# One transfer for each tile of tokens, and a new order of the first loads

## The chip, the cores and the metric

The kernel runs on one core of one Trainium2 chip. The metric is the time on the device, in microseconds (us); smaller is better.

## What is computed

The input is x, 2048 tokens of 576 numbers. Each token is normalized (mean 0, variance 1, 1e-5 added under the root) to xn. The output adds three things:

```python
xn = _layernorm(x, axis=-1)
return x + _A_ref(xn, ...) + _B_ref(xn, w1, w2)
# _B_ref: h = silu(xn @ w1)      w1 is 576 x 4608
#         out = h @ w2           w2 is 4608 x 576
# _A_ref: K[d,l] = Re(sum_n C dB exp(dt A l)), 128 states for each d
#         y = causal convolution of xn with K over the 2048 tokens, + xn * Dskip
```

All is float32. The kernel writes float32 operands of TensorE as a high and a low part (`xh`, `xl`; `w1h`, `w1l`; `gh`, `gl`) and multiplies high by high, high by low and low by high.

## The kernel before, in words

**Tiles of tokens.** The 2048 tokens are 16 tiles `j` of 128. A tile is not a run of neighbours: token number = 64 n + (16 times a quarter) + j, with n from 0 to 31 and four quarters. A tile in SBUF has 128 partitions, 32 for each quarter. In DRAM the 32 rows of one quarter lie 64 tokens apart, and the four quarters 16 tokens apart. `quarters` (L73) yields the four quarters with the queue that each is to use; `load_x` (L163) and `store` (L175) issue one transfer of 32 rows for each. Tiles 0 and 1 are loaded one by one, from SyncE's (SP) and ScalarE's (ACT) queues in turn, the others in pairs `j, j+1` of 4.6 KB a row.

**The feed-forward part** (`ffn`, L242) runs over two halves of the tokens (tiles 0 to 7, 8 to 15), nine chunks of 512 of the 4608 hidden columns, and two blocks of four tiles. `up` (L303) multiplies w1 into 128 hidden columns at a time, ScalarE applies silu (`gf`) and makes `gh`, VectorE (DVE) makes `gl`; `down` (L323) multiplies w2 and DVE adds to the accumulator `acc` (L346), which starts as x itself. `load_w1` (L250) fetches 256 columns of w1 as `w1r`: rows 0 to 511 in one transfer (L257) and rows 512 to 575 twice, to both halves of the partitions (L258, L259). For the very first columns it cuts these three in two by columns, for the two queues. `split_w1` (L271) makes `w1h` on ScalarE (L279) and `w1l` on DVE (L281). The last seven chunks of the second half use a Winograd-like scheme (`wino_ffn`, L468).

**The convolution** is done beside it, as a generator `side` (L1050) that `weave` interleaves with `ffn`: phase 0 (load, `norm`, transpose), the table of K (`natural`, `kgen`), a transform (`spread`, `spectral`) through DRAM buffers `d1u`, `d1k`, `d2`, and at the end `conv` (L1032), which adds the result to a tile: for tiles 0 to 7 through `yt` and an adding store, for tiles 8 to 15 into the same PSUM bank as the last `down`.

**Order.** Each engine runs its instructions in order. A scheduler in the framework sets the order from the code and from hints: `behind(ins)` puts an instruction behind another, `tc.high_priority()` pulls it forward. `norm` (L180) holds tile 1's statistics (`bn_stats`, L188) behind tile 0's normalized tile (`pins["xn"]`). Each queue issues its transfers in order.

**The end.** After the last `down`, pairs 8, 10 and 12 and the tiles 14 and 15 are stored from the two queues (L1111 to L1114).

Of the kernel before, what the change touches and what calls it, by code (L numbers as in the profile page):

```python
# [13 lines left out]
ALU = mybir.AluOpType  # L14
# [3 lines left out]
P = 128  # L18
# [4 lines left out]
NJ = 16  # L23
NKT = 4
HD = D // 2
# [16 lines left out]
def kernel(  # L42
# [21 lines left out]
    nc = tc.nc  # L64
# [2 lines left out]
    WINO_C = 2  # L67


    xv = x.rearrange("b (n q2 q1 j) d -> q1 q2 n (b j) d", q2=2, q1=2, j=NJ)  # L70
    ov = out.rearrange("b (n q2 q1 j) d -> q1 q2 n (b j) d", q2=2, q1=2, j=NJ)

    def quarters(v, engines):  # L73

        for q in range(4):
            yield slice(32 * q, 32 * q + 32), v[q // 2, q % 2], engines[q % len(engines)]

    dram = ctx.enter_context(tc.tile_pool(name="dram", bufs=1, space=DRAM))
    d1u = dram.tile([32 * P, D], F32, name="d1u")
# [10 lines left out]
    s4 = None  # L90
# [19 lines left out]
    acc = {}  # L110
# [21 lines left out]
    pairs = {}  # L132
    held = []
    pins = {}
    wino = {}

    def behind(ins):
        return tc.issue_after(ins) if ins is not None else nullcontext()

    def spread(up):  # L140

        s1 = up.tile([P, 2, P], F32R, name="s1", bufs=1)
        nc.gpsimd.dma_start(s1, cs1)
        for j in range(NJ):
            src = up.tile([P, D], F32, tag="xr", name="xr")
            nc.sync.dma_start(src, dxn[:, j])
            for m in range(2):
                lo, hi = slice(64 * m, 64 * m + 64), slice(64 - 64 * m, 128 - 64 * m)
                u1 = up.tile([P, D], F32, tag="u1", name="u1")
                sp = up.tile([P, D], F32R, tag="sp", name="sp")  # L150
                nc.scalar.copy(sp[lo, :], src[lo, :])
                nc.vector.tensor_sub(sp[hi, :], src[lo, :], sp[lo, :])
                for h in range(2):
                    hs = slice(h * HD, (h + 1) * HD)
                    pu = pss.tile([P, 512], F32, tag="pss", name="pu")
                    nc.tensor.matmul(pu[:, :HD], s1[:, 0, :], sp[:, hs], start=True, stop=False)
                    nc.tensor.matmul(pu[:, :HD], s1[:, 1, :], sp[:, hs], start=False, stop=True)
                    nc.scalar.copy(u1[:, hs], pu[:, :HD])  # L158
                nc.gpsimd.dma_start(  # L159
                    d1u.rearrange("(p m j) d -> m j p d", m=2, j=NJ)[m, j], u1)  # L160
                yield j

    def load_x(j, pool, tag, engines):  # L163

        t = pool.tile([P, 2, D], F32, tag=tag, name=f"{tag}{j}")
        for i in range(j, j + 2, 1 if j == 0 else 2):
            for ps, v, eng in quarters(xv, engines):
                if j == 0:
                    eng.dma_start(t[ps, i], v[:, i])
                else:  # L170
                    eng.dma_start(t[ps], v[:, j:j + 2])
        pairs[j] = t
        return t[:, 0, :], t[:, 1, :]

    def store(t, j, engines, **more):  # L175

        for ps, v, eng in quarters(ov, engines):
            eng.dma_start(v[:, j:j + 2] if len(t.shape) > 2 else v[:, j], t[ps], **more)

    def norm(p0, js, xs):  # L180

        n = len(js)
        st = p0.tile([P, 2, 2, 6], F32, tag="st", name="st")
        mv = p0.tile([P, 2, 2], F32, tag="mv", name="mv")
        for i in range(n):
            for h in range(2):
              with behind(pins["xn"] if js[0] == 1 else None):
                nc.vector.bn_stats(out=st[:, i, h, :], in_=xs[i][:, h * HD:(h + 1) * HD])  # L188
            nc.vector.bn_aggr(out=mv[:, i, :], in_=st[:, i, :, :])
        sd = p0.tile([P, 2], F32, tag="sd", name="sd")  # L190
        mb = p0.tile([P, 2], F32, tag="mb", name="mb")
        nc.vector.tensor_scalar(sd[:, :n], mv[:, :n, 1], 1e-5, None, op0=ALU.add)
        pins["sd"] = nc.gpsimd.tensor_tensor(sd[:, :n], sd[:, :n], mhalf[:, :n], op=ALU.pow).ins
        xn = p0.tile([P, 2, D], F32, tag="xn", name="xn") if js[0] < 8 else pairs[js[0]]
        for i, j in enumerate(js):
            if j % 2 == 0 or j < 4:
                pins["xn"] = nc.vector.tensor_scalar(xn[:, i, :], xs[i], mv[:, i, 0:1], sd[:, i:i + 1],
                                                 op0=ALU.subtract, op1=ALU.mult).ins
            else:
                nc.vector.scalar_tensor_tensor(mb[:, i:i + 1], mv[:, i, 0:1], -1.0, sd[:, i:i + 1],  # L200
                                               op0=ALU.mult, op1=ALU.mult)
                pins["xo"] = nc.scalar.activation(xn[:, i, :], xs[i], AF.Identity,
                                                  scale=sd[:, i:i + 1], bias=mb[:, i:i + 1]).ins
        return xn

    def phase0(p0, js):
        j0 = js[0]
        if j0 < 8:
            xs = load_x(j0, accp, "acc", (nc.sync, nc.scalar) if j0 == 0 else (nc.sync,))
            acc.update(zip(js, xs))  # L210
            yield
        else:
            xs = load_x(j0, p0, "xj", (nc.sync,))
        if j0:
            with behind(pins["xt1"] if j0 == 2 else None):
                turned(p0, js, norm(p0, js, xs))
        else:
            xn = [norm(p0, (j,), (xj,)) for j, xj in zip(js, xs)]
            last = pins["xn"]
            for j in js:  # L220
                turned(p0, (j,), xn[j], None if j else last)
                pins[f"xt{j}s"] = pins["xt_s"]
# [19 lines left out]
    def ffn():  # L242
# [7 lines left out]
        def load_w1(half, c, t):  # L250

            f = c * FT + t
            first = half == 0 and c == 0
            r1 = (pa if first and t else w1x if t and w1x else wp).tile([P, 5, 2 * P], F32, tag="w1r", name="w1r", bufs=1)
            for eng, a, e in ((nc.scalar, 0, P), (nc.sync, P, 2 * P)) if first and t == 0 else ((nc.sync, 0, 2 * P),):
                fs = slice(f * P + a, f * P + e)
                eng.dma_start(r1[:, 0:4, a:e], w1[0:512, fs].rearrange("(k p) f -> p k f", p=P))  # L257
                eng.dma_start(r1[0:64, 4, a:e], w1[512:576, fs])  # L258
                pins["load"] = eng.dma_start(r1[64:128, 4, a:e], w1[512:576, fs]).ins  # L259
            R1[half, c, t] = r1  # L260

        def need_w1(half, c, t):
# [60 lines left out]
        def down(blk, jj, terms=None):  # L323
# [22 lines left out]
                    nc.vector.tensor_add(acc[j][:, hs], po[:, :HD], acc[j][:, hs])  # L346
            if half == 0 and c == NCH - 1:
                if j % 2:
                    store(pairs[j - 1], j - 1, (nc.gpsimd,))
                    acc[7 + j], acc[8 + j] = load_x(7 + j, accp, "acc", (nc.gpsimd,))  # L350

        def next_xt(b):
            xt = new_xt(2 + b)
# [628 lines left out]
    def tail():  # L982

        def last(j):
            y = yp.tile([P, 2, D], F32, tag="yt", name="yt", bufs=2)
            py = [[pool.tile([P, 512], F32, tag=tag, name="py") for pool, tag in pools]
                  for pools in (((ps2, "ps2"), (pss, "pss")), ((pss, "pss"),) * 2)]
            conv((j, j + 1), py)
            for i in range(2):
                for h in range(2):  # L990
                    nc.scalar.copy(y[:, i, h * HD:(h + 1) * HD], py[i][h][:, :HD])
                conv_load(j + i + AHEAD)
            store(y, j, (nc.gpsimd,), accum_op=ALU.add)

        steps = [(tail_at[0] + j * tail_at[1], conv_load, j) for j in range(AHEAD)]
        steps += [(tail_at[2] + j * tail_at[3], last, j) for j in range(0, 8, 2)]
        for at, f, j in sorted(steps, key=lambda v: v[0]):
            yield at
            with behind(pins["load"]):
                f(j)  # L1000
# [31 lines left out]
    def conv(js, banks):  # L1032

        ys = [yss.pop(j) for j in js]
        first = pins["pe"]
        for n in range(8 * len(js)):
            i, q1, q2, h = n // 8, n // 4 % 2, n // 2 % 2, 1 - n % 2
            o = 64 * q1 + 32 * q2
            rows = slice(64 * h, 64 * h + 64)
            with tc.high_priority() if n else nullcontext(), behind(first):  # L1040
                mm = nc.tensor.matmul(banks[i][h][o:o + 32, :HD], s4[rows], ys[i][rows, 2 * q2 + q1],
                                      start=True, stop=True, tile_position=(64 * h, o), skip_group_check=True)
            if n == 0:
                first = mm.ins
# [64 lines left out]
        next(g)  # L1109
    weave(fg, 276, sd)  # L1110
    for j in range(8, 14, 2):  # L1111
        store(pairs[j], j, (nc.sync, nc.scalar))
    for j in (14, 15):
        store(acc[j], j, (nc.sync, nc.scalar))  # L1114


def _hi_lo(a):
# [75 lines left out]
```

## Time and profile before

| what | value |
|---|---|
| time, median of 3 runs | 1107.63 us (1107.56 to 1108.49) |
| time of the profiled execution | 1108.0 us, of which the span of its instructions is 1106.1 |
| TensorE (PE) busy | 1089.5 us, 98% of the span |
| VectorE (DVE) / ScalarE (ACT) / GpSimd (POOL) busy | 950.6 / 722.6 / 141.5 us |
| granted TensorE clock | 0.999 |
| moved by transfers | 173.67 MB, mean 157 GB/s |

PE's busy share leaves out the start, where it waits for the first data, and the end, where only stores run. A busy PE is not a PE at its peak: ends of matmuls are modelled and overlap.

### The profile page before, as it was taken

The page shows a single profiled execution, that of the slowest core. Times are in us where ns is not written, and L with a number is a line of the kernel's source. Part 1 is how long each engine was busy: PE and PEld are TensorE (multiplying, and loading weights), DVE is VectorE, ACT ScalarE, POOL GpSimd, SP SyncE. Part 2 cuts the span into 40 slices and gives each one's busy share as a digit, 9 for nine tenths or more (in the row PEclk, how much of TensorE's full clock was granted, in tenths as well). Part 3 has the DMA queues.
Part 4 walks back from the last instruction along what each step waited for, and adds up shares of the span by engine and source line. Part 5 has one row for each costly group of instructions (what it writes and reads, how often), then busy time and mean ns, then how long its engine had stood idle before and what let it go on. Part 6 is the DMA issues. An engine that isn't in the chain of part 4 may idle for free.

```text
span 1106.1 us, 23074 instructions
## 1 busy us (share of the span) xinstructions
PE 1089.5 (98%) x9101; PEld 986.5 (89%) x9101; DVE 950.6 (86%) x1615; ACT 722.6 (65%) x1283; POOL 141.5 (13%) x246
## 2 busy tenths in 40 slices
PE   6999999999999999999999999999999999999998
PEld 5989999898998888898999899999999998999787
DVE  6699989999999999999999997988888888886323
ACT  4475457677777676767667656877778777785320
POOL 1112100000000000000330001111111111111220
PEclk9999999999999999999999999999999999999999
DMA  8536552355263535457974246456545655554984
GB/s 261 157 123 205 168 165 94 118 149 153 84 176 108 138 125 132 154 120 254 240 196 89 84 92 193 146 167 179 158 152 176 182 173 150 177 161 109 248 216 111
DMA packets 163100, 173.67 MB, mean 157 GB/s; under 512 B 88608, under 2 KB 128816, under 8 KB 162352
## 3 DMA queue, kind: packets, MB, share of 16 engines
q1 hardware_dynamic: 137360, 105.02, 34.6%
q0 software_dynamic: 24272, 65.38, 19.4%
q10 hardware_dynamic: 1360, 1.80, 0.7%
q8 instruction: 72, 1.18, 0.5%
q14 instruction: 36, 0.29, 0.1%
HBM read 109.64 MB, written 62.60 MB: 156 GB/s over the span
## 4 chain that ended last, share of the span: by engine, by line
PE 78%; DVE 12%; ACT 3%; DMA 3%; issue 2%; SPq 0%; POOL 0%; ACTq 0%; DVEq 0%
PE po L341 34%; PE ph L311 16%; PE pb L468 6%; PE pc L468 3%; PE kp L888 2%; PE pk L1022 2%; PE pb L1022 2%; PE pu L1022 2%; PE pa L468 2%; PE ph L313 1%; PE ph L312 1%; PE z L903 1%; DMA kl<-d1k 1%; DVE acc L346 1%; DVE th L829 1%
## 5 line engine op out<-in xcount | busy, mean ns | idle before, releaser
L341 PE MATMUL po<-w,gh 128*128 128x288 f32 x2304 | 474.3, 296 | 0.7 <-DVE acc L346 0.7
L341 PEld LDWEIGHTS po<-w,gh 128*128 128x128 f32 x2304 | 375.1, 188 | 16.6 <-issue 3.3
L341 PE MATMUL po<-w,gl 128*128 128x288 f32 x1152 | 333.5, 295 | 0.0
L341 PEld LDWEIGHTS po<-w,gl 128*128 128x128 f32 x1152 | 214.9, 188 | 1.7
L346 DVE TENSOR_TENSOR acc<-po,acc 128x288 f32<-128x288 f32 x296 | 129.8, 451 | 54.5 <-PE po L341 53.2
L311 PE MATMUL ph<-xh,w1h 128*128 128x512 f32 (+1 forms) x368 | 99.7, 388 | 1.4 <-ACT gf L319 1.0
L311 PE MATMUL ph<-xl,w1h 128*128 128x512 f32 (+1 forms) x368 | 98.2, 384 | 0.0
L311 PE MATMUL ph<-xh,w1l 128*128 128x512 f32 (+1 forms) x368 | 98.0, 383 | 0.0
L319 ACT ACTIVATE gf<-ph 128x512 f32<-128x512 f32 (+1 forms) x92 | 53.0, 579 | 51.3 <-PE ph L313 31.5
L311 PEld LDWEIGHTS ph<-xl,w1h 128*128 128x128 f32 x368 | 68.0, 191 | 13.4
L311 PEld LDWEIGHTS ph<-xh,w1l 128*128 128x128 f32 x368 | 66.6, 189 | 12.0
L311 PEld LDWEIGHTS ph<-xh,w1h 128*128 128x128 f32 x368 | 65.0, 191 | 11.7 <-ACT gf L319 1.6
L845 ACT ACTIVATE c<-th,magic 128x1040 f32<-128x1040 f32 x36 | 42.0, 1168 | 40.6 <-DVE C L866 26.5
L159 POOL DMA_DIRECT2D d1u<-u x32 | 17.6, 550 | 393.9 <-ACT u L158 392.5
L847 ACT ACTIVATE c<-th 128x1040 f32<-128x1040 f32 x36 | 38.7, 1074 | 40.7 <-DVE th L846 40.6
L321 DVE TENSOR_TENSOR gl<-gf,gh 128x512 fp32r<-128x512 f32 (+1 forms) x92 | 60.3, 658 | 3.8 <-ACT gh L320 3.6
L927 POOL DMA_DIRECT2D m<-in_cm_dram x64 | 34.0, 533 | 216.0 <-PE pu L1022 135.8
L320 ACT CAST gh<-gf 128x512 fp32r<-128x512 f32 (+1 forms) x92 | 55.1, 602 | 8.7 <-PE po L341 7.7
L485 DVE TENSOR_TENSOR gl<-gf,gh 128x512 fp32r<-128x512 f32 x56 | 37.8, 688 | 23.4 <-ACT gh L484 23.0
L865 DVE TENSOR_TENSOR S<-th,C 128x1024 f32<-128x1024 f32 x36 | 43.8, 1218 | 7.4 <-ACT th L848 7.3
L846 DVE SCALAR_TENSOR_TENSOR th<-c,th 128x1040 f32<-128x1040 f32 x36 | 44.3, 1232 | 0.3 <-ACT c L845 0.3
L829 DVE TENSOR_TENSOR th<-vt,fT 128x1040 f32<-128x1040 f32 x36 | 44.3, 1233 | 0.2
(269 smaller groups left out, 2371.0 us busy)
## 6 DMA issues: line engine op xcount, KB each, us to landing
w1r<-in_B_w_dram SPq DMA_DIRECT2D x35, 512.0 KB, 3.9
dw<-w SPq DMA_DIRECT2D x28, 576.0 KB, 4.8
w<-dw POOLq DMA_DIRECT2D x28, 576.0 KB, 5.9
w2r<-in_B_w_dram SPq DMA_DIRECT2D x44, 288.0 KB, 4.8
d1u<-u POOLq DMA_DIRECT2D x32, 288.0 KB, 2.9
d1k<-stage SPq DMA_DIRECT2D x18, 512.0 KB, 6.5
ul<-d1u SPq DMA_DIRECT2D x32, 288.0 KB, 3.0
kl<-d1k SPq DMA_DIRECT2D x32, 288.0 KB, 3.6
```

Of the source, the lines that this page charges most:

```text
L311: nc.tensor.matmul(ph, w[:, kt, :], v[:, kt, a:e], start=n + kt == 0, stop=False)
L319: nc.scalar.activation(gf, ph, AF.Silu)
L320: pins["gh"] = nc.scalar.copy(gh, gf).ins
L321: pins["gl"] = nc.vector.tensor_sub(gl, gf, gh).ins
L341: pins["pe"] = nc.tensor.matmul(po[:, :HD], gs[g][:, js], ws[:, w, hs], start=n == 0 and j not in begun, stop=n == 3 * len(terms) - 1, ski ...
L346: nc.vector.tensor_add(acc[j][:, hs], po[:, :HD], acc[j][:, hs])
L468: pins["pe"] = nc.tensor.matmul(dst, a[:, kt], v[:, kt], start=start and n == 0, stop=stop and n == 5, skip_group_check=True).ins
L829: nc.vector.tensor_mul(split(th), row(vt[:, 0:65], 65), col(fT, i, 65))
L845: nc.scalar.activation(c65, th, AF.Identity, bias=magic)
L846: nc.vector.scalar_tensor_tensor(th, c65, MAGIC, th, op0=ALU.subtract, op1=ALU.subtract)
L865: nc.vector.tensor_mul(ov3, t[:, :, 0:64].rearrange("n d (x y) -> n d x y", y=32), mv3)
L1022: nc.tensor.matmul(dst, st, mv[:, hs], start=n == 0, stop=n == 3 * len(terms) - 1)
```

## The change

It replaces the four quarter transfers of a tile by one, renumbers the quarters so that they stand in natural order, and so changes the patterns of `d1u` and `conv` (same rows, same bytes). It takes the first loads off ScalarE's queue, brings the last 64 rows of w1 to both halves of the partitions by one transfer that reads them twice, places tile 1's statistics behind tile 0's variance, and stores the last tiles whole from ScalarE's queue, tile 15 in two halves by columns from two queues.

```diff
-    xv = x.rearrange("b (n q2 q1 j) d -> q1 q2 n (b j) d", q2=2, q1=2, j=NJ)
-    ov = out.rearrange("b (n q2 q1 j) d -> q1 q2 n (b j) d", q2=2, q1=2, j=NJ)
-    def quarters(v, engines):
-        for q in range(4):
-            yield slice(32 * q, 32 * q + 32), v[q // 2, q % 2], engines[q % len(engines)]
+    xv = x.rearrange("b (n q j) d -> q n (b j) d", q=4, j=NJ)
+    ov = out.rearrange("b (n q j) d -> q n (b j) d", q=4, j=NJ)
...
-                    d1u.rearrange("(p m j) d -> m j p d", m=2, j=NJ)[m, j], u1)
+                    d1u.rearrange("(e m q j) d -> m j e q d", m=2, q=2, j=NJ)[m, j], u1)
...
-    def load_x(j, pool, tag, engines):
+    def load_x(j, pool, tag, eng):
         t = pool.tile([P, 2, D], F32, tag=tag, name=f"{tag}{j}")
-        for i in range(j, j + 2, 1 if j == 0 else 2):
-            for ps, v, eng in quarters(xv, engines):
-                if j == 0:
-                    eng.dma_start(t[ps, i], v[:, i])
-                else:
-                    eng.dma_start(t[ps], v[:, j:j + 2])
+        if j == 0:
+            for i in range(2):
+                eng.dma_start(t[:, i], xv[:, :, i])
+        else:
+            eng.dma_start(t, xv[:, :, j:j + 2])
...
-    def store(t, j, engines, **more):
-        for ps, v, eng in quarters(ov, engines):
-            eng.dma_start(v[:, j:j + 2] if len(t.shape) > 2 else v[:, j], t[ps], **more)
+    def store(t, j, eng, **more):
+        eng.dma_start(ov[:, :, j:j + 2] if len(t.shape) > 2 else ov[:, :, j], t, **more)
...
-              with behind(pins["xn"] if js[0] == 1 else None):
-                nc.vector.bn_stats(out=st[:, i, h, :], in_=xs[i][:, h * HD:(h + 1) * HD])
+                with behind(pins["var"] if js[0] == 1 else None):
+                    nc.vector.bn_stats(out=st[:, i, h, :], in_=xs[i][:, h * HD:(h + 1) * HD])
...
-        nc.vector.tensor_scalar(sd[:, :n], mv[:, :n, 1], 1e-5, None, op0=ALU.add)
+        pins["var"] = nc.vector.tensor_scalar(sd[:, :n], mv[:, :n, 1], 1e-5, None, op0=ALU.add).ins
...
-            for eng, a, e in ((nc.scalar, 0, P), (nc.sync, P, 2 * P)) if first and t == 0 else ((nc.sync, 0, 2 * P),):
-                fs = slice(f * P + a, f * P + e)
-                eng.dma_start(r1[:, 0:4, a:e], w1[0:512, fs].rearrange("(k p) f -> p k f", p=P))
-                eng.dma_start(r1[0:64, 4, a:e], w1[512:576, fs])
-                pins["load"] = eng.dma_start(r1[64:128, 4, a:e], w1[512:576, fs]).ins
+            fs = slice(f * P, (f + 2) * P)
+            eng = nc.sync
+            eng.dma_start(r1[:, 0:4, :], w1[0:512, fs].rearrange("(k p) f -> p k f", p=P))
+            pins["load"] = eng.dma_start(r1[:, 4, :], w1[512:576, fs].unsqueeze(0).broadcast_to([2, 64, 2 * P])).ins
...
-    for j in range(8, 14, 2):
-        store(pairs[j], j, (nc.sync, nc.scalar))
-    for j in (14, 15):
-        store(acc[j], j, (nc.sync, nc.scalar))
+    for j in range(8, 14, 2):
+        store(pairs[j], j, nc.scalar)
+    store(acc[14], 14, nc.scalar)
+    for h, eng in enumerate((nc.scalar, nc.sync)):
+        hs = slice(h * HD, (h + 1) * HD)
+        eng.dma_start(ov[:, :, 15, hs], acc[15][:, hs])
```

How the rows stand in a queue shows the change best. SP's first transfers before; a row names the tile and the tensor it comes from, and the shape written (`acc_104` holds tiles 0 and 1, `acc_171` tiles 2 and 3, `acc_252` 4 and 5, `acc_299` 6 and 7, `w2r` 128 rows of w2):

```order
L169 DMA acc_104<-in_A_u_dram 32x576 x4
L257 DMA w1r<-in_B_w_dram 128x4x128
L258 DMA w1r<-in_B_w_dram 64x128
L259 DMA w1r<-in_B_w_dram 64x128
L257 DMA w1r<-in_B_w_dram 128x4x256
L258 DMA w1r<-in_B_w_dram 64x256
L259 DMA w1r<-in_B_w_dram 64x256
L171 DMA acc_171<-in_A_u_dram 32x1152 x4
L288 DMA w2r<-in_B_w_dram 128x576 x4
L171 DMA acc_252<-in_A_u_dram 32x1152 x4
L171 DMA acc_299<-in_A_u_dram 32x1152 x4
L257 DMA w1r<-in_B_w_dram 128x4x256
```

And now, the same place (`acc_160` holds tiles 2 and 3, `acc_238` 4 and 5, `acc_282` 6 and 7, `xj` the tiles from 8 on):

```order
L163 DMA acc_104<-in_A_u_dram 128x1x576 x2
L249 DMA w1r<-in_B_w_dram 128x4x256
L250 DMA w1r<-in_B_w_dram 128x1x256
L249 DMA w1r<-in_B_w_dram 128x4x256
L250 DMA w1r<-in_B_w_dram 128x1x256
L165 DMA acc_160<-in_A_u_dram 128x1x1152
L279 DMA w2r<-in_B_w_dram 128x576 x4
L165 DMA acc_238<-in_A_u_dram 128x1x1152
L165 DMA acc_282<-in_A_u_dram 128x1x1152
L165 DMA xj_600<-in_A_u_dram 128x1x1152
L165 DMA xj_749<-in_A_u_dram 128x1x1152
L1072 DMA vt<-in_cv_dram 128x69
```

Both tiles, both pieces of w1 and tiles 2 and 3 are now seven transfers in one queue; the four tiles from 8 on stand ahead of the next chunk's w1 (before they stood behind it).

DVE's first rows before, from tile 0's variance to the statistics of tiles 2 and 3 (`st`, `mv`, `sd` are the statistics; rows that name `pt` split a transposed tile):

```order
L192 TENSOR_SCALAR sd<-mv 128x1
L197 TENSOR_SCALAR xn<-acc_104,mv,sd 128x576
L188 BN_STATS st<-acc_104 128x6 x2
L189 BN_AGGR mv<-st 128x2
L192 TENSOR_SCALAR sd<-mv 128x1
L197 TENSOR_SCALAR xn<-acc_104,mv,sd 128x576
L125 TENSOR_TENSOR xl_147<-pt,xh_146 128x4x128
L129 TENSOR_TENSOR x_0_148<-pt_156,x_0_148 64x128
L125 TENSOR_TENSOR xl_147<-pt,xh_146 128x4x128
L129 TENSOR_TENSOR x_0_148<-pt_167,x_0_148 64x128
L281 TENSOR_TENSOR w1l<-w1r,w1h 128x640 x4
L188 BN_STATS st<-acc_171 128x6 x4
```

And now, from the row behind tile 0's variance:

```order
L180 BN_STATS st<-acc_104 128x6 x2
L189 TENSOR_SCALAR xn<-acc_104,mv,sd 128x576
L181 BN_AGGR mv<-st 128x2
L184 TENSOR_SCALAR sd<-mv 128x1
L189 TENSOR_SCALAR xn<-acc_104,mv,sd 128x576
L120 TENSOR_TENSOR xl_136<-pt,xh_135 128x4x128
L124 TENSOR_TENSOR x_0_137<-pt_145,x_0_137 64x128
L120 TENSOR_TENSOR xl_136<-pt,xh_135 128x4x128
L124 TENSOR_TENSOR x_0_137<-pt_156,x_0_137 64x128
L272 TENSOR_TENSOR w1l<-w1r,w1h 128x640
L180 BN_STATS st<-acc_160 128x6 x4
L272 TENSOR_TENSOR w1l<-w1r,w1h 128x640 x3
```

Tile 1's statistics moved ahead of tile 0's normalized tile, as asked; the scheduler also moved the statistics of tiles 2 and 3 ahead of three of the four low parts of w1.

The end of ScalarE's queue before (SP's ends with the same four rows of stores; `acc_6463` is pair 8, `acc_6528` pair 10, `acc_6868` pair 12, `acc_7052` tiles 14 and 15):

```order
L484 CAST gh<-gf 128x512 x2
L178 DMA out_dram<-acc_6463 32x1152 x2
L178 DMA out_dram<-acc_6528 32x1152 x2
L178 DMA out_dram<-acc_6868 32x1152 x2
L178 DMA out_dram<-acc_7052 32x576 x4
```

And now, where SP keeps one row alone, the second half of tile 15:

```order
L475 CAST gh<-gf 128x512 x2
L170 DMA out_dram<-acc_6410 4x32x1152
L170 DMA out_dram<-acc_6469 4x32x1152
L170 DMA out_dram<-acc_6801 4x32x1152
L170 DMA out_dram<-acc_6979 4x32x576
L1107 DMA out_dram<-acc_6979 4x32x288
```

A store that was two rows in each of two queues is one row in one; its shape on the DRAM side has 4 as its first number, where it had 32.

More of the change, by code (lines that the diff above doesn't have):

```diff
@@ L208, in phase0 @@
         if j0 < 8:
-            xs = load_x(j0, accp, "acc", (nc.sync, nc.scalar) if j0 == 0 else (nc.sync,))
+            xs = load_x(j0, accp, "acc", nc.sync)
             acc.update(zip(js, xs))
@@ L212, in phase0 @@
         else:
-            xs = load_x(j0, p0, "xj", (nc.sync,))
+            xs = load_x(j0, p0, "xj", nc.sync)
         if j0:
@@ L348, in down @@
                 if j % 2:
-                    store(pairs[j - 1], j - 1, (nc.gpsimd,))
-                    acc[7 + j], acc[8 + j] = load_x(7 + j, accp, "acc", (nc.gpsimd,))
+                    store(pairs[j - 1], j - 1, nc.gpsimd)
+                    acc[7 + j], acc[8 + j] = load_x(7 + j, accp, "acc", nc.gpsimd)
         def next_xt(b):
@@ L992, in last @@
                 conv_load(j + i + AHEAD)
-            store(y, j, (nc.gpsimd,), accum_op=ALU.add)
+            store(y, j, nc.gpsimd, accum_op=ALU.add)
         steps = [(tail_at[0] + j * tail_at[1], conv_load, j) for j in range(AHEAD)]
@@ L1036, in conv @@
         for n in range(8 * len(js)):
-            i, q1, q2, h = n // 8, n // 4 % 2, n // 2 % 2, 1 - n % 2
-            o = 64 * q1 + 32 * q2
+            i, q, h = n // 8, n // 2 % 4, 1 - n % 2
+            o = 32 * q
             rows = slice(64 * h, 64 * h + 64)
             with tc.high_priority() if n else nullcontext(), behind(first):
-                mm = nc.tensor.matmul(banks[i][h][o:o + 32, :HD], s4[rows], ys[i][rows, 2 * q2 + q1],
+                mm = nc.tensor.matmul(banks[i][h][o:o + 32, :HD], s4[rows], ys[i][rows, q],
                                       start=True, stop=True, tile_position=(64 * h, o), skip_group_check=True)
```

## The prediction

> **What bounds the kernel now.** I read the page first, then the waits of PE, then the chain of waits, and last the timeline and the transfers at both ends. From the page:
>
> ```profile
> span 1106.1 us, 23074 instructions
> PE 1089.5 (98%) x9101; PEld 986.5 (89%) x9101; DVE 950.6 (86%) x1615; ACT 722.6 (65%) x1283; POOL 141.5 (13%) x246
> ```
>
> PE has work for all but 16.6 us. The waits of PE (us in total, times, longest) say where those lie:
>
> ```profile
> PE pt L122 <- DVE xn L197: 8.0, 2, 6.9
> PE ph L311 <- ACT gf L319: 1.0, 3, 0.6
> PE pt L127 <- DVE xl L125: 0.9, 1, 0.9
> ```
>
> Eight are waits for the first normalized tiles; nothing else is over 1. So the change can only act on the start, on the end behind PE's last matmul, or by making a new wait between them. The chain of waits through the start (start, length):
>
> ```profile
> 1.27 2.90 DMA acc<-in_A_u_dram
> 4.29 0.83 DVE st L188 x2
> 6.24 0.03 DVE xn L197
> 6.73 0.82 DVE st L188 x2
> 8.66 0.59 DVE xn L197
> 9.29 1.13 PE pt L122 x4
> 10.45 0.59 ACT xh L123
> 11.08 4.38 PE ph L311 x20
> ```
>
> Tile 0 has landed at 4.17, tile 1's normalized tile follows at 8.66, and `up` starts at 11.08. Rows of the timeline beside it:
>
> ```profile
> 9.59 0.72 ACT L279 CAST w1h<-w1r 128x640 fp32r<-128x640 f32 x1 [0.82 <-DMA w1r<-in_B_w_dram]
> 12.10 3.03 DVE L281 TENSOR_TENSOR w1l<-w1r,w1h 128x640 fp32r<-128x640 f32 x4
> 15.05 1.53 DVE L188 BATCH_NORM_STATS2 st<-acc 128x6 f32<-128x288 f32 x4
> 15.54 0.64 PE L311 MATMUL ph<-xh,w1l 128*128 128x256 f32 x4
> 16.76 0.64 PE L311 MATMUL ph<-xl,w1h 128*128 128x256 f32 x4
> 23.30 2.98 DVE L188 BATCH_NORM_STATS2 st<-acc 128x6 f32<-128x288 f32 x8
> 26.20 1.41 DVE L299 TENSOR_TENSOR w<-w2r,w 128x576 fp32r<-128x576 f32 x2
> ```
>
> Data is there just ahead of use, and PE takes the second low part of w1 at 15.54.
>
> **How a transfer is spread.** All turns on one thing that the trace shows in part. ACT's queue (q10) carries few transfers, so its packets can be counted:
>
> ```profile
> q10 hardware_dynamic: 1360, 1.80, 0.7%
> out_dram<-acc ACTq DMA_DIRECT2D x6, 144.0 KB, 3.6
> acc<-in_A_u_dram ACTq DMA_DIRECT2D x4, 72.0 KB, 3.1
> out_dram<-acc ACTq DMA_DIRECT2D x4, 72.0 KB, 2.3
> w1r<-in_B_w_dram ACTq DMA_DIRECT2D x1, 256.0 KB, 5.0
> w1r<-in_B_w_dram ACTq DMA_DIRECT2D x2, 32.0 KB, 4.5
> ```
>
> Runs of data: 14 transfers of 32 rows, one of 128 rows with 4 pieces, two of 64 rows: 448 + 512 + 128 = 1088. Of the 1360 packets 272 are left, which is 17 transfers times 16. I read this as one closing packet on each of the 16 DMA engines: a transfer of 32, 64 or 128 rows is cut along its rows into 16 equal shares. Every pattern of before has such a number as its slowest dimension. The new ones do not: a tile's 128 tokens are 4 quarters 16 tokens apart, of 32 rows 64 tokens apart, which is no single dimension, so the DRAM side of a load or store is 4 x 32 rows; and the last 64 rows of w1, read twice, are 2 x 64. If the cut still goes along the slowest dimension, it gives 4 shares and 2, and a transfer runs on 4 or 2 of the 16 engines. If it goes along the 128 partitions of the tile, nothing is lost. No row of before shows it; these are the two ends. I take the first, because the shares of before follow the rows of the pattern whatever the size, and a pattern is walked from its slowest dimension.
>
> The Trainium skill, page "DMA: Bandwidth & Descriptors", section "Why a DMA increments its semaphore by 16 and not by 1", says that the number of engines is the largest up to 16 that divides the slowest dimension other than 1 of both patterns. By that rule the loads and stores get 4 engines, the doubled rows 2, and the sum is the one below; with 16 it would be 1105.3. By that rule, the trace agrees as far as it goes (272 = 17 x 16); no run here shows a smaller number.
>
> **What one engine moves.** From the transfers of 1.7 to 4.0 us, and the best slice of the first 30 us (40 slices):
>
> ```profile
> q1 hardware_dynamic: 162, 0.27, 45.7%
> q10 hardware_dynamic: 152, 0.24, 32.5%
> GB/s 0 0 126 308 241 210 125 283 312 150 229 296 210 212 320 240 178 243 320 360 323 335 224 221 237 258 234 320 406 424 401 335 384 382 311 249 239 203 234 246
> ```
>
> 0.51 MB in 78.2% of 16 engines times 2.3 us is 17.7 KB/us for each; 424 GB/s over 16 is 26.5. In the first stretch two queues share an engine; after the change one queue has it, so I take 24, nearer the upper end.
>
> **The start, step by step,** on the engine that serves both the tiles and the doubled rows (closing left out). Traffic begins at 1.8 (third slice of 0.75 us). A tile is 295 KB, 74 on each of 4 engines, 3.1 us: tile 0 in at 4.9, tile 1 at 7.9 (before: 4.17, and 5.5 or so). The first w1 piece is 33 KB a share (1.4) and 66 KB of doubled rows on each of 2 engines (2.7): 12.0. The second piece: 16.1. Tiles 2 and 3, 590 KB, 147 a share, 6.1: 22.3. Four w2 pieces at 0.8: 25.3. Tiles 4 and 5: 31.5; 6 and 7: 37.6.
>
> What waits: DVE's statistics of tile 1 now stand ahead of tile 0's xn, so both wait for tile 1; `up` starts near 14, 3 late. That is soon swallowed: the statistics of tiles 2 and 3 now stand behind the first low part of w1, and the other three low parts are queued behind them. 22.3 + 1.5 (statistics) + 0.8 (a quarter of 3.03) = 24.6, against 15.54 for the matmul that wants it: 9.1 late. Next, PE has then stood for about 6 us. At the start its first 20 matmuls took 4.38 us, later ones 0.64 for 4 less overlap, about 0.12 each; if it must start slowly again, that is 2 more. Last, the statistics of tiles 4 to 7 (23.30 before) come at 32.4 and find 4 and 5 but wait from 33.9 to 37.6 for 6 and 7, with the low parts of w2 (26.20) queued behind; half of that reaches PE, 2. Start: 13. The bounds: at 26.5 KB/us and without the two additions 7; at 17.7, with them, 25. Below 7 the engines' number must be other than 4. The freed ACT queue and the earlier tile-1 statistics gain nothing here: the transfers are late.
>
> **Between.** Each later w1 load has its doubled rows on 2 engines: 2.7 us in place of two 64-row transfers on 16 (8 KB a share, 0.35), so 2.4 later. It counts only where a load is waited for; the chain shows two such places behind the start:
>
> ```profile
> 61.05 3.37 DMA w1r<-in_B_w_dram
> 297.25 3.60 DMA w1r<-in_B_w_dram
> ```
>
> I take 2 x 2.4 = 5; bounds 0 (all covered) and 8 chunks x 2.4 = 19. The patterns of `d1u` and `conv` move the same rows as before; their slowest dimension is 64, so 0. POOL's stores and reloads of tiles are issued fewer to one queue that is busy 13% of the time; their later landing is covered by tens of us. If the adding stores of `yt` crowd the `ys` loads, up to 5 more.
>
> **The end.** DVE's last sums and SP's stores:
>
> ```profile
> 1096.69 0.46 DVE L346 TENSOR_TENSOR acc<-po,acc 128x288 f32<-128x288 f32 x1 [0.34 <-PE po L341]
> 1099.65 0.46 DVE L346 TENSOR_TENSOR acc<-po,acc 128x288 f32<-128x288 f32 x1 [0.35 <-PE po L341]
> 1101.24 0.46 DVE L346 TENSOR_TENSOR acc<-po,acc 128x288 f32<-128x288 f32 x1 [0.35 <-PE po L341]
> 1084.92 17.79 SPq L178 DMA_DIRECT2D out_dram<-acc  x10
> 1092.64 10.07 SPq L178 DMA_DIRECT2D out_dram<-acc  x8
> ```
>
> Pair 8 goes out at 1084.9, pair 10 at 1092.6, pair 12 at 1097.2, tile 14 at 1100.1, tile 15 by 1101.7. On 4 engines a pair takes 6.1, a tile 3.1. With 1.1 from issue to traffic (0.75 to 1.8 at the start): 1086.0 to 1092.1; 1093.7 to 1099.8; pair 12 waits for that, to 1105.9; tile 14 to 1109.0; tile 15 to 1112.1. Before, the last bytes went at about 1104, 2 ahead of the span's end, so the end is 8 later. Stores alone, 1086 to 1104, bound it:
>
> ```profile
> q10 hardware_dynamic: 479, 1.18, 28.2%
> q1 hardware_dynamic: 461, 1.10, 22.6%
> ```
>
> 2.28 MB in 50.8% of 16 x 18 us is 15.6 KB/us: by that 20 later; at 26.5, 7.
>
> **Sum.** 13 + 5 + 8 = 26 on a span of 1106.1, so 1132 and 1134 with the 1.9 around it. The profiled execution was 1108.0, the median 1107.63; against the median 1133.
>
> **Rivals.** *Sixteen shares after all: faster.* Then tile 0 (295 KB at 16 x 17.7) is in at 2.9 plus closing, some 0.9 ahead of 4.17; tile 1's statistics begin when tile 0's variance ends and no more at 6.73, and its xn 0.5 earlier (8.66): 1.4 at the start. At the end one issue (0.45, from 10.07 for 8 and their waits) and half the bytes of tile 15 go: 0.9. 1107.6 - 2.3 = 1105.3. It decides from the point where tile 1 lands before 5.5. For it: more rows a transfer, fewer issues. The skill's page, section "Rules for kernel authors", says to use one 128-partition transfer in place of halves; by that the time is this rival's, 1105.3. Against it: the 4 and 2 above. *Four shares, but the start covered* (an engine over 26.5 KB/us with few others at work, PE slowed by little): only the end stays, 1107.6 + 8 = 1115.6. For it: fewer than 16 engines leave more of the memory to each. Against: tiles 2 and 3 alone would need 10 us less.
>
> **How the numbers follow.** Forecast 0.70 (its own range 1118 to 1150: start 7 to 20, between 0 to 8, end 7 to 12, not all at one end); everything at the slow bounds, over 1150, 0.04; the covered start 0.10 (1112 to 1118); sixteen shares 0.16. The range 1112 to 1150 leaves out 0.16 and 0.04. A measurement of this kernel tells about 0.2% (2.2 us) from no change; the gain of 2.3 lies on that line, so 0.16 falls half to faster, half to same.
>
> **What would show it.** Right: in the transfers, the first tile's landing at about 5 and tile 1's at 8, w1's doubled rows landing some 2.5 behind the rest; DVE's third group of statistics waiting on a transfer until past 20; PE waiting 5 us or more for the low part of w1; stores still moving 7 us or more behind DVE's last sum. Wrong: tile 1 in by 5.5, `up` starting before 11, the last store done within 2.5 of the last sum.

## The result, and the profile after

The changed kernel takes 1191.24 us (median of 6, 1190.43 to 1199.73) against 1107.82 for the kernel before (median of 6): a ratio of 1.0763, 95% interval 1.0734 to 1.0793. The direction is the forecast's; the loss is 83 us where 25 were forecast, and the time lies above the range.

The page of the changed kernel, the lines that answer to those shown of before:

```profile
span 1189.1 us, 22898 instructions
PE 1106.4 (93%) x9101; PEld 998.2 (84%) x9101; DVE 951.0 (80%) x1615; ACT 719.8 (61%) x1283; POOL 125.6 (11%) x210
q1 hardware_dynamic: 135584, 104.60, 31.3%
q10 hardware_dynamic: 660, 2.21, 0.5%
```

PE does the same 9101 matmuls, waits 66 us more, and its busy time grew by 16.9. The queue of ScalarE (q10) settles what the prediction had to bound: it now carries five transfers of 128 rows, 640 runs of data, and 20 of the 660 packets are left. With one closing packet for each engine, as the prediction read the row of before, that is 5 times 4: a tile goes out on 4 engines. The same bytes were moved (173.67 MB in both).

PE's waits (us in total, times, longest), of which before had the second with 8.0 and none of the others:

```profile
PE po L332 <- DVE acc L337: 23.2, 9, 6.5
PE pt L117 <- DVE xn L189: 13.4, 2, 13.2
PE ph L302 <- DVE w1l L272: 9.3, 1, 9.3
PE pc L459 <- ACT w1h L376: 4.2, 1, 4.2
PE po L332 <- DMA w<-dw: 3.9, 2, 2.3
```

Only the last is a wait of PE's own for a transfer. The first is the largest and runs through a second engine: PE waits for VectorE's sums, and VectorE stands in order behind something else that waits for a transfer, itself or through ScalarE.

The start, from the timeline (start, length, engine, operation, idle time before it):

```profile
7.96 0.82 DVE L180 BATCH_NORM_STATS2 st<-acc 128x6 f32<-128x288 f32 x2 [7.03 <-DMA acc<-in_A_u_dram]
11.83 0.82 DVE L180 BATCH_NORM_STATS2 st<-acc 128x6 f32<-128x288 f32 x2 [2.61 <-DMA acc<-in_A_u_dram]
16.99 1.22 PE L302 MATMUL ph<-xh,w1h 128*128 128x256 f32 x4 [0.86 <-ACT xh L118]
28.59 1.54 DVE L180 BATCH_NORM_STATS2 st<-acc 128x6 f32<-128x288 f32 x4 [9.76 <-DMA acc<-in_A_u_dram]
30.05 2.28 DVE L272 TENSOR_TENSOR w1l<-w1r,w1h 128x640 fp32r<-128x640 f32 x3
30.91 1.23 PE L302 MATMUL ph<-xh,w1l 128*128 128x256 f32 x4 [9.31 <-DVE w1l L272]
```

The chain is the predicted one, link for link: statistics of tiles 2 and 3 wait for their load, three low parts of w1 stand behind them, PE takes the second low part at 30.91 where it took it at 15.54 before. The prediction had 24.6.

To see where the rest went, take VectorE's 296 sums `acc` in order of time and compare the n-th with the n-th of before. The delay is flat between the steps listed here:

| sum number | 1 | 41 | 137 | 169 | 257 | 296 | end of span |
|---|---|---|---|---|---|---|---|
| before, at us | 32.5 | 179.7 | 550.3 | 665.4 | 998.5 | 1101.2 | 1106.1 |
| after, later by | 22.0 | 39.5 | 40.7 | 58.1 | 64.3 | 72.3 | 83.0 |

So, in before's time: the start 22; 17 to 18 between 80 and 180 us; 17 in the switch of halves (550 to 665 us), 4 to 6 spread behind it; 8 at the adding stores of `yt`; 11 behind the last sum.

### The profile page after: what moved, and what is told of

Same layout as the page of the kernel before. It is cut to its first block, busy times and chain, and to the rows that moved or that the text cites. A ratio compares the mean times of both kernels' runs of the same rounds, so it can differ in the third digit from the quotient of the medians.

```text
span 1189.1 us, 22898 instructions
## 1 busy us (share of the span) xinstructions
PE 1106.4 (93%) x9101; PEld 998.2 (84%) x9101; DVE 951.0 (80%) x1615; ACT 719.8 (61%) x1283; POOL 125.6 (11%) x210
## 2 busy tenths in 40 slices
DMA packets 164654, 173.67 MB, mean 146 GB/s; under 512 B 90676, under 2 KB 130500, under 8 KB 163908
## 3 DMA queue, kind: packets, MB, share of 16 engines
q0 software_dynamic: 28304, 65.40, 17.9%
q10 hardware_dynamic: 660, 2.21, 0.5%
## 4 chain that ended last, share of the span: by engine, by line
issue 39%; PE 37%; DMA 11%; DVE 4%; POOL 3%; ACT 2%; SPq 2%; POOLq 0%; DVEq 0%; ACTq 0%
PE po L332 16%; PE pb L459 5%; PE pc L459 3%; DMA acc<-in_A_u_dram 2%; PE ph L302 2%; DMA w<-dw 2%; DMA xj<-in_A_u_dram 2%; PE pu L1013 2%; PE pk L1013 2%; PE pb L1013 2%; DMA kl<-d1k 2%; PE pa L459 1%; POOL d1u L154 1%; DMA out_dram<-acc 1%; PE pc L465 1%
## 5 line engine op out<-in xcount | busy, mean ns | idle before, releaser
L332 PE MATMUL po<-w,gh 128*128 128x288 f32 x2304 | 482.8, 299 | 29.6 <-DVE acc L337 23.2
L332 PEld LDWEIGHTS po<-w,gh 128*128 128x128 f32 x2304 | 380.6, 190 | 48.7 <-DVE acc L337 25.9
L332 PEld LDWEIGHTS po<-w,gl 128*128 128x128 f32 x1152 | 217.4, 190 | 1.7
L310 ACT ACTIVATE gf<-ph 128x512 f32<-128x512 f32 (+1 forms) x92 | 52.9, 578 | 60.2 <-PE ph L304 39.5
L302 PEld LDWEIGHTS ph<-xh,w1h 128*128 128x128 f32 x368 | 65.9, 194 | 16.6 <-ACT gf L310 3.9
L476 DVE TENSOR_TENSOR gl<-gf,gh 128x512 fp32r<-128x512 f32 x56 | 37.8, 688 | 25.5 <-ACT gh L475 25.1
L998 DVE TENSOR_TENSOR kl<-kl,kh 128x576 fp32r<-128x576 f32 x32 | 24.2, 756 | 25.9 <-ACT kh L997 23.8
```

The lines of the kernel that those rows point to most:

```text
L302: nc.tensor.matmul(ph, w[:, kt, :], v[:, kt, a:e], start=n + kt == 0, stop=False)
L310: nc.scalar.activation(gf, ph, AF.Silu)
L332: pins["pe"] = nc.tensor.matmul(po[:, :HD], gs[g][:, js], ws[:, w, hs], start=n == 0 and j not in begun, stop=n == 3 * len(terms) - 1, ski ...
```

## The experiments

The theory: tiles run on 4 engines and w1's doubled rows on 2. The rival: the engines do not matter; one queue for all first loads and the new order of tile 1's statistics hold up the start, and the later steps follow from it. Each median below stands beside 1107.99, 1108.78 or 1108.48 for before in the same set of runs; the changed kernel is 1191.24.

**Transfers on 16 engines again, in several forms.** Quarters, in the changed kernel's queue and place (the stores are cut in the same way, which is not shown):

```diff
-            eng.dma_start(t, xv[:, :, j:j + 2])
+            for q in range(4):
+                eng.dma_start(t[32 * q:32 * q + 32], xv[q, :, j:j + 2])
...
-            pins["load"] = eng.dma_start(r1[:, 4, :], w1[512:576, fs].unsqueeze(0).broadcast_to([2, 64, 2 * P])).ins
+            for p in (0, 64):
+                pins["load"] = eng.dma_start(r1[p:p + 64, 4, :], w1[512:576, fs]).ins
```

> After with every tile moved as four quarters of 32 rows again (all four in the queue that the changed kernel uses), and the last rows of w1 as two transfers of 64 rows; the order of the first loads in one queue, whole w1 pieces and tile 1's statistics behind tile 0's variance stay. If the 83 us come from transfers on 4 or 2 of the 16 engines, all of it goes: 1104 to 1112 us. If they come from the one queue and the new order of statistics, the time stays above 1150 us.

One transfer a tile, of 128 rows in one dimension:

```diff
-    xv = x.rearrange("b (n q j) d -> q n (b j) d", q=4, j=NJ)
-    ov = out.rearrange("b (n q j) d -> q n (b j) d", q=4, j=NJ)
+    xv = x.rearrange("b (p j) d -> p (b j) d", j=NJ)
+    ov = out.rearrange("b (p j) d -> p (b j) d", j=NJ)
```

> After with one transfer for each tile, but the 128 tokens of a tile lie 16 tokens apart in one dimension of 128 rows, not in 4 x 32 (so the convolution sees its tokens in another order; number of instructions, bytes and run lengths are unchanged). The last rows of w1 are still read twice by one transfer. If the number of engines follows the slowest dimension, tiles run on 16 engines and only w1's doubled rows on 2 are left: 1106 to 1122 us. If a transfer of 128 rows is slow as such, or the queue and the order are, above 1150 us.

The same, and w1's last rows in two transfers (the second edit of the first run):

> As the run before (tiles by one transfer of 128 rows in one dimension), and w1's last rows by two transfers of 64 rows; TensorE's instructions stand in the same order as in the changed kernel. By the engines: the sixteen-shares rival of the prediction, 1103 to 1110 us. By the queue and the order: above 1150 us.

Only w1's last rows in two transfers, tiles as in the changed kernel:

> After with w1's last rows by two transfers of 64 rows and nothing else; every engine's order but SyncE's is that of the changed kernel. By the prediction's step (2 x 2.4 us for later loads, and about 5 of the start's 22), 1178 to 1190 us. If the doubled rows are the main cause, below 1150; if they are always covered, 1190 to 1192.

| run | median us | ratio to before, 95% interval | first sum later by | last sum later by |
|---|---|---|---|---|
| quarters, w1 in two | 1109.39 | 1.0015, 1.0006 to 1.0025 | 3.5 | 2.4 |
| 128 rows, w1 doubled | 1129.18 | 1.0193, 1.0175 to 1.0211 | 5.0 | 21.9 |
| 128 rows, w1 in two | 1105.64 | 0.9977, 0.9968 to 0.9986 | -0.7 | -1.2 |
| 4 x 32 rows, w1 in two | 1169.53 | 1.0556, 1.0539 to 1.0572 | 17.6 | 52.7 |

The rival falls with the third row. It has the one queue, the order of the statistics at the start, one transfer a tile, and TensorE's instructions in the changed kernel's order. What differs is the walk through DRAM, the two transfers for w1's last rows, and three pairs of neighbouring instructions of VectorE, at the statistics of the later tiles, that changed places; 85.6 us are gone. Where the rows lie in DRAM is not the cause either: the first row reads and writes the changed kernel's very rows. That first run says nothing of the order, though: with its quarters the scheduler put VectorE's second low part of w1 ahead of the statistics of tiles 2 and 3 again, and from the switch of halves on it reordered TensorE too. The doubled rows cost 21.7 us (1191.24 - 1169.53) beside slow tiles and 23.5 (1129.18 - 1105.64) beside fast ones, the slow tiles 62 to 64. The second and the fourth row miss their bounds by 7 and 8 us, both because the doubled rows are dearer than expected. The first lies within its own, but loses 1.4: its eight quarter loads of tiles 0 and 1 occupy SyncE's queue for 3.64 us (1.37 for two whole tiles), and the first sum is 3.5 later. That the one brings the other is likely, and was not tested:

```profile
0.75 3.64 SPq L165 DMA_DIRECT2D acc<-in_A_u_dram  x8
```

Queue rows of the kernel of 128 rows, first with w1 doubled, then in two, and last that of 4 x 32 rows with w1 in two:

```profile
q1 hardware_dynamic: 135704, 104.60, 32.6%
q10 hardware_dynamic: 720, 2.21, 0.5%
```

```profile
q1 hardware_dynamic: 136784, 104.61, 33.5%
```

```profile
q1 hardware_dynamic: 136664, 104.61, 31.9%
```

The five tile stores now leave 80 closing packets, 5 x 16. Between the first two, q1 differs by 1080 packets at the same runs of data: 36 loads of w1, each with 32 closing packets in place of 2. Between the last two, by 120: ten tile transfers in SyncE's queue, 16 in place of 4. So 4 and 2 are counted, not only inferred. The Trainium skill, page "DMA: Bandwidth & Descriptors", section "Why a DMA increments its semaphore by 16 and not by 1", gives this number as the largest up to 16 that divides the slowest dimension of both patterns; these rows agree (128 gives 16, 4 x 32 gives 4, 2 x 64 gives 2).

**The changed kernel with one place repaired.** Five runs take one group of tile transfers each back to 16 engines. Two use quarters in the same place of the queue (the load edit above, for tiles 0 to 7 or for tiles 8 to 15), one the old lines of the last stores, and two, for GpSimd's queue, rows in one dimension as above, since quarters there would have moved TensorE's order. In these two the same bytes move, but the rows of those transfers stand in another order than the rest of the kernel takes them, so what they compute is not the function above; only their times count here. The start:

> After, and only tiles 0 to 7 are loaded as four quarters each, in the same queue and place. If the start's 22 us are the 4 engines, 15 to 18 go and w1's doubled rows keep about 5: 1173 to 1177 us. If they are the one queue and tile 1's statistics ahead of tile 0's normalized tile, it stays at 1188 to 1192.

The loads of tiles 8 to 15 for the convolution:

> After, and only the four later loads (tiles 8 to 15, xj) go as four quarters each, in the same place of SyncE's queue. VectorE's statistics waited 8.0 and 2.9 us for them and TensorE then 6.5 us for VectorE's sums. If it is those loads, 7 to 12 us of the 18 between 85 and 190 us go: 1179 to 1184 us. If the 18 us are all w1's doubled rows, 1190 to 1192.

The switch of halves:

```diff
-            eng.dma_start(t, xv[:, :, j:j + 2])
+            eng.dma_start(t, xr[:, j:j + 2] if eng is nc.gpsimd else xv[:, :, j:j + 2])
...
+        if eng is nc.gpsimd and not more:
+            eng.dma_start(orr[:, j:j + 2], t)
```

> After, and only GpSimd's four stores and four reloads between the halves (tiles 0 to 7 out, tiles 8 to 15 in) take a tile's rows as one dimension of 128 (16 apart), so in those transfers the rows stand in another order; every other engine's order is unchanged. If these eight transfers on 4 engines cause what grows between 550 and 640 us of before's time, some 18 to 20 us go: 1170 to 1174 us. By the prediction's step (their landing is covered), 1189 to 1192.

The adding stores:

```diff
+        if more:
+            eng.dma_start(orr[:, j:j + 2], t, **more)
```

> After, and only GpSimd's four adding stores of yt take a tile's rows as one dimension of 128 (so those rows stand in another order); every engine's order is kept. If the 8 to 10 us that grow between 1000 and 1100 us of before's time are these stores on 4 engines ahead of GpSimd's loads of w (TensorE waits 2.3 for w, ScalarE 6.3 for yt's buffer), 1180 to 1184 us. If they come of something else, above 1188.

The last stores:

```diff
-    for j in range(8, 14, 2):
-        store(pairs[j], j, nc.scalar)
-    store(acc[14], 14, nc.scalar)
+    for t, j in [(pairs[j], j) for j in (8, 10, 12)] + [(acc[j], j) for j in (14, 15)]:
+        for q in range(4):
+            eng = (nc.sync, nc.scalar)[q % 2]
+            eng.dma_start(ov[q, :, j:j + 2] if len(t.shape) > 2 else ov[q, :, j], t[32 * q:32 * q + 32])
```

> After, and only the last stores (tiles 8 to 15) go out as before: quarters from two queues. The prediction gave the end 8 us, the trace shows 11 behind the last sum: 1179 to 1183 us if 4 engines are the cause. If the queue was never the limit at the end, 1190 to 1192.

| repaired | median us | ratio to before, 95% interval | gained | the prediction's price |
|---|---|---|---|---|
| tiles 0 to 7 at the start | 1179.06 | 1.0646, 1.0625 to 1.0668 | 12.2 | in its 13 for the start |
| loads of tiles 8 to 15 | 1184.45 | 1.0686, 1.0670 to 1.0703 | 6.8 | none |
| switch of halves | 1176.17 | 1.0616, 1.0600 to 1.0632 | 15.1 | 0 |
| adding stores of `yt` | 1182.62 | 1.0668, 1.0652 to 1.0684 | 8.6 | up to 5 |
| last stores | 1183.06 | 1.0678, 1.0659 to 1.0697 | 8.2 | 8 |
| w1's doubled rows | 1169.53 | 1.0556, 1.0539 to 1.0572 | 21.7 | 5, and a part of the start |

The six gains add up to 72.6 of the 85.6 between the changed kernel and that of 128 rows: what one place loses is partly hidden while another still does. The runs of the start and of the switch gained 2 us less than the least expected, that of tiles 8 to 15 0.5 less and that of the last stores 0.1; at the start the quarters may bring back the 3.5 seen above. The run of the start is not pure: VectorE's second low part of w1 now stands behind the first of the four statistics of tiles 2 and 3 and no more behind all four, which by these rows (start, length) is worth 1.1 of the gain (1.54 - 0.46); the statistics themselves begin at 20.48 in place of 28.59:

```profile
20.48 0.46 DVE L187 BATCH_NORM_STATS2 st<-acc 128x6 f32<-128x288 f32 x1 [5.64 <-DMA acc<-in_A_u_dram]
20.86 0.81 DVE L279 TENSOR_TENSOR w1l<-w1r,w1h 128x640 fp32r<-128x640 f32 x1
```

In each run the delay by VectorE's sums is gone where the theory put it: the first sum is 8.2 late in place of 22.0 with the start repaired, and from sum 137 to sum 169 the delay stays (40.8 to 40.6) with the switch of halves repaired. In the changed kernel VectorE meets the loads of tiles 8 to 15 between 85 and 190 us of its own time, with PE behind it; before it waited 1.3 us for them:

```profile
DVE st L180 <- DMA xj<-in_A_u_dram: 10.9, 2, 8.0
```

**Why does the switch of halves cost 15?** No engine but GpSimd waits there for a tile. A wait of ScalarE in the changed kernel from 570 to 660 us:

```profile
ACT u L153 <- DMA d1u<-u: 20.4, 2, 11.0
```

and GpSimd's queue beside it:

```profile
582.92 0.71 POOL L170 DMA_DIRECT2D out_dram<-acc  x1
594.99 0.65 POOL L165 DMA_DIRECT2D acc<-in_A_u_dram  x1 [11.36 <-DMA out_dram<-acc]
595.63 0.65 POOL L154 DMA_DIRECT2D d1u<-u  x1
```

GpSimd stands for 11.4 us for its tile store to land before it may reload the buffer, the store of `u` stands behind it, and ScalarE, in order, waits for the buffer of `u`. In the kernel before, GpSimd stood for at most 4.8 us there, and ScalarE never waited for that buffer:

```profile
548.78 1.94 POOL L171 DMA_DIRECT2D acc<-in_A_u_dram  x4 [4.83 <-DMA out_dram<-acc]
```

That was the next theory: GpSimd's order. Its test gives the six stores of `u` to SyncE:

```diff
-                nc.gpsimd.dma_start(
+                (nc.sync if 12 <= j < 15 else nc.gpsimd).dma_start(
```

> After, and the six stores of u to d1u that fall into the switch of halves are issued from SyncE's queue and not from GpSimd's; the tile stores and reloads stay on 4 engines. If the loss there is a chain (GpSimd stands in order for a tile's store to land, the store of u stands behind it, ScalarE waits for u's buffer), most of the 18 to 20 us go: 1170 to 1180 us, and the wait of ScalarE for the transfer of u (9.4 and 11.0 us) is gone. If it is the reloaded tiles that come late for VectorE's sums, or contention of the transfers, it stays within 3 us of 1191.

1192.09 us (1.0756, 1.0740 to 1.0773): nothing gained, so GpSimd's order alone is not the cause. ScalarE's wait is still there, and the rows of SyncE show why (the wait from 560 to 665 us, then the queue):

```profile
ACT u L153 <- DMA d1u<-u: 12.8, 1, 12.8
```

```profile
585.87 0.62 SPq L907 DMA_DIRECT2D d1k<-stage  x1
586.54 9.25 SPq L862 DMA_DIRECT2D d1k<-stage  x1
595.88 10.04 SPq L154 DMA_DIRECT2D d1u<-u  x1
606.02 1.56 SPq L249 DMA_DIRECT2D w1r<-in_B_w_dram  x1
```

SyncE has nothing to do with the tile stores, and yet two issues take it 9 and 10 us. In the kernel before, the issue of `d1k` and the one behind it, there that of `w1r`, took 3.95 and 3.45:

```profile
545.14 3.95 SPq L871 DMA_DIRECT2D d1k<-stage  x1
549.19 3.45 SPq L257 DMA_DIRECT2D w1r<-in_B_w_dram  x1
```

That points at the engines: while 4 of them work off a tile for 11 us, every transfer with a share on them waits. To test that alone, transfers that nothing waits for were added to the kernel of 128 rows with w1 in two, eight in all, once on 4 engines and once on 16, with every instruction of the two in the same order:

```diff
+                if m == 1 and 3 <= j < 11:
+                    with behind(last):
+                        nc.scalar.dma_start(extra[j - 3], x.rearrange("b (n q j) d -> q n (b j) d", q=4, j=NJ)[:, :, 8:10])
```

> The kernel of tiles in one dimension of 128 rows and w1's last rows in two transfers, with eight extra transfers of 590 KB (DRAM to DRAM, 4 x 32 rows) from ScalarE's otherwise empty queue, one at every second store of u, that nothing waits for. They take 4 engines for 7 us or more each. If other transfers with a share on those engines wait for them, the time is 8 to 40 us over the next run's. If only the wait for a transfer's own landing costs, within 2 us of it.

> As the run before, but the extra transfers read the rows as one dimension of 128, so on 16 engines; all instructions stand in the same order. The measure for the run before: 1105 to 1115 us.

1128.52 us (1.0171, 1.0150 to 1.0193) against 1114.30 (1.0053, 1.0036 to 1.0070): 14.2 us between eight transfers on 4 engines and the same eight on 16, though no instruction waits for either: 1.8 each. The packets bear the engines out: each transfer moved for 7.5 to 8.4 us in the first run and for 2.2 to 3.1 in the second, and the eight left 32 and 128 closing packets. Issuing them took ScalarE about the same, 0.62 and 0.50 us each. The waits of ScalarE from 250 to 560 us, with 4 engines and then with 16:

```profile
ACT w L293 <- DMA w2r<-in_B_w_dram: 28.5, 6, 12.5
```

```profile
ACT w L293 <- DMA w2r<-in_B_w_dram: 8.7, 4, 5.4
```

ScalarE waits up to 12.5 us for w2, whose loads have 128 rows, where it waited up to 5.4 with the foreign transfer on 16 engines. Eight tile transfers in the switch of halves cost 15.1, about the same. That the mechanism is the one in the switch is inferred from this; how much of the 15.1 is the reloads' own landing was not separated.

## Why the prediction was wrong, step by step

*How a transfer is spread: right.* It chose 4 and 2 engines between two ends of which no row of before showed either; the closing packets count them.

*The rival of sixteen shares: right in size.* It gave 1105.3; the kernel that makes it true took 1105.64, 2.3 less than before. That the parts fit is in part luck: the working had 1.4 at the start and 0.9 at the end, and in the trace the first sum is 0.7 earlier, the last 1.2, and the span ends 3.3 behind it in place of 4.9. So the new order and the whole stores do gain a little, but only where whole tiles run on 16 engines: with quarters in one queue the kernel lost 1.4. Of the runs that keep the order of the tokens none was faster than the kernel before.

*The start: the right chain, mis-sized, 22 for 13.* By matching instructions of PE and VectorE its three terms were 15.4 for 9.1 (the second low part of w1, 30.91 against 15.54), 1.7 for 2 (the slow restart of PE: behind its 9.3 us of waiting, groups of four matmuls took 1.05 us, and 0.64 only 4 us later), and 4.9 for 2 (the low parts of w2 behind the statistics of tiles 6 and 7, which waited until 46.73 and not 37.6):

```profile
46.73 1.54 DVE L180 BATCH_NORM_STATS2 st<-acc 128x6 f32<-128x288 f32 x4 [4.84 <-DMA acc<-in_A_u_dram]
```

What was mis-sized in the first term is the rate of an engine. The prediction let it serve its transfers one after the other at 24 KB/us and had tiles 2 and 3 in at 22.3; they were in by 28.6. The order is borne out: the trace does not name the engine of a packet, but from 22 us on packets follow each other without a gap in four rows, and in each w2's 32 packets begin only when its share of tiles 2 and 3 is done, at 24.4 and 25.1 us in two of them and at 27.4 and 28.0 in the other two, which came later to it. By the prediction's own shares the busiest engine had then moved 492 KB (148 for tiles 0 and 1, 66 and 131 for the two pieces of w1 and their doubled rows, 147 for tiles 2 and 3) between 2.2 and 28.0: 19.1 KB/us. The 24 held only at the end, when few engines were at work: packets of 4.6 KB took 0.19 us each from 22 to 28 us, 24 KB/us, and w1's packets of 1 KB 0.067 up to 22 us, 15 KB/us. Tile 0 came at 7.96 and not 4.9; which packets of tile 1 and w1 went between its own was not taken apart.

*Between: this is where it failed, 50 for 5.* The delay grew from 22.0 at the first sum to 72.3 at the last. The 5 for w1 counted two loads that someone waited for, 2.4 each, and its bound of 19 eight, of 34 that follow the start. The doubled rows cost 21.7 to 23.5, of which some 5 lie in the start. Between the first and the 41st sum alone they made 10: with fast tiles the first sum was 5.0 later than before, the 41st 14.8. ScalarE's waits for `w1r` in the whole run of the kernels of 128 rows, with w1's rows doubled and then in two:

```profile
ACT w1h L270 <- DMA w1r<-in_B_w_dram: 10.7, 4, 4.5
```

```profile
ACT w1h L271 <- DMA w1r<-in_B_w_dram: 1.3, 2, 0.9
```

So four loads were waited for and not two, up to 4.5 us; where the rest of the 23.5 arises was not taken apart. The four loads of tiles 8 to 15 had no price at all: 6.8, with VectorE waiting 10.9 us for two of them. The adding stores of `yt` had up to 5, outside the sum: 8.6. GpSimd's stores and reloads were put at 0 because their later landing was covered by tens of us: 15.1. That landing was not covered for GpSimd itself, which stood for 11 to 13 us for each store, and giving the stores of `u` to SyncE gained nothing. The step that failed is this pricing: it counted for a transfer on few engines only who waits for that transfer, left out one group of them, and gave nothing for who waits behind it on the same engines. The last is shown by the pair of added transfers, 1.8 us each; for w1's doubled rows it stays open.

*The end: 8 forecast, 8.2 gained by undoing it.* That the two agree so closely is in part luck. The span ended 15.6 us behind the start of the last sum, where before it was 4.9, so 10.7 later; undone, it was 4.4 again, but the last sum came 1.9 later. The stores ran so:

```profile
1157.19 15.75 ACTq L170 DMA_DIRECT2D out_dram<-acc  x4
1173.49 0.46 DVE L337 TENSOR_TENSOR acc<-po,acc 128x288 f32<-128x288 f32 x1 [0.34 <-PE po L332]
```

```profile
q10 hardware_dynamic: 660, 2.21, 16.6%
```

2.21 MB in 16.6% of 16 x 39 us is 21.3 KB/us for an engine, a little under the 24 taken.

## What to carry to other kernels

Before merging transfers, write down the slowest dimension of both patterns: four transfers of 32 rows, each on 16 engines, became one on 4. A transfer on few engines must be priced twice, by its own landing and by every other transfer that has a share on those engines; a cover of tens of us for its own landing says nothing of the second. And the queue of an engine that is busy 13% of the time can still cost 15 us, most likely by the time for which its transfers hold engines that others need.

## What the runs showed of the hardware

- A transfer of 590 KB that nothing waits for cost 1.8 us more of the whole on 4 engines than on 16, by the pair of runs above.
- Single issues of SyncE took up to 10 us while 4 engines worked off the tiles of another queue (11.6 in the changed kernel), where in the kernel before, those in the same place took up to 3.95.
- Stalls cost PE more than their length, as the groups of 1.05 us behind its longest wait show. Its busy time grew by 16.9 of the 83 us with the same matmuls, and the granted clock fell only where it had waited (core 0: stretch, its length, PE busy, PEld, DVE, ACT, POOL, clock, DMA share, GB/s):

```profile
85.00:190.00 105.00, 93.26 (x540) 82.40 (x539) 78.61 (x141) 50.40 (x77) 15.10 (x17) 0.95 0.50 167
190.00:570.00 380.00, 374.74 (x3852) 337.45 (x3851) 367.56 (x541) 258.83 (x386) 17.90 (x30) 1.00 0.45 134
570.00:660.00 90.00, 78.86 (x813) 70.94 (x812) 69.81 (x103) 50.34 (x77) 8.75 (x15) 0.91 0.51 138
```

The Trainium skill, page "TensorE: Matmul & The Clock Gate", section "HAM oscillation — how this bites in real kernels", says that waits of some 3.4 us let the clock fall and that the next work then runs slow; the clock of 0.91 around the waits of up to 4.9 us in the switch, and 1.00 in the stretch before it, agree.
- GpSimd's tile transfers do not show their engines by closing packets. The packets in flight fit 4 again: from 575 to 640 us of the changed kernel, 4 and 8 were the commonest numbers of 4.6 KB packets of its queue that moved together (12.1 and 8.3 us; nine or more for 2), and 16 (8.4 us) with the switch repaired, from 560 to 625 us. Besides, each of its twelve tile transfers showed 384 packets more on 4 engines than on 16 (q0 has 28304 packets in the changed kernel, 25232 with eight of them repaired, 26768 with four). What these packets are stays open.
